# Joined bundles of small matmuls, and a table of steps for the scheduler's ranks, in a fused memory-attention and feed-forward kernel

## The chip, the cores and the metric

The kernel runs on one core of one Trainium2 chip. The metric is the device time of one execution in microseconds (us), the median of several runs. Five engines matter: TensorE (PE in the profile; PEld is its weight load), VectorE (DVE), ScalarE (ACT), GpSimd (POOL) and the queue that issues DMAs (SP).

## What is computed

```python
a = phi - max(phi, axis=seq); a = exp(a); a = a / sum(a, axis=seq)
k_m = einsum('bhsm,bhsd->bhmd', a, k)          # 32 memories per head
v_m = einsum('bhsm,bhsd->bhmd', a, v)
scores = softmax(q @ k_m.T / sqrt(64), axis=m)
x = scores @ v_m                               # then heads side by side: 4608 x 512
h = x @ w_in                                   # 512 -> 2048
g = h * erf(softplus(h))
out = g @ w_out                                # 2048 -> 512
```

There are 8 batches, 8 heads, 576 positions, 64 numbers per head, 32 memories; all is float32.

## The kernel before

**The work and its steps.** Since `scores @ v_m @ w_in` can be grouped the other way, the kernel never forms `x`: it multiplies `v_m` by `w_in` first. Per batch there are these kinds of work on PE. `sums` (in `one_memory`, L548) are 40 matmuls that make `k_m` and `v_m` of a batch (80, in two bundles, in batch 0); a transposition (`turn`, L582) follows. `heads` (L605) makes two things out of 64-row, 32-column pieces: `scores` of one half of a batch's positions (`attention`, two per batch, 8 matmuls of 288 columns) and `vw`, that is `v_m` times 512 columns of `w_in` (four per batch, 8 matmuls of 512 columns; eight of 256 columns in batch 0). These three are the *small* bundles; they are exact float32, and each of their matmuls stands twice in the profile. The wide work is `ffn1` (L710: one half of 288 positions of one 128-row slice of `h`, 6 matmuls) and `ffn2` (L794: one 128-row tile of the output, 3 matmuls for each of 16 slices of `g`). A *step* is one slice of `h`; there are 16 per batch, 128 in all. 64 positions of each batch do not fill a tile of 128; they go through DRAM (`rest_d`) and two batches' rests make one tile, `psr` (`ffn2_rest`).

**Numbers in two parts.** Most products are float32 in three passes, with each operand split into a high and a low part (`split`, L360: ACT writes the high part, DVE subtracts for the low part, `vw_lo`, `at_lo`, `wo`). The first steps use exact float32 matmuls instead: ffn1 in the first 4 steps (`psh<-at`), ffn2 in the first 8 (`pso<-w`).

**Around PE.** ffn1's result goes from PSUM to `h` by a copy of DVE (L725; ACT may take it in the first 16 steps, L726). ACT makes softplus and erf in groups of steps, each with a table load (L733, L738). DVE multiplies `e` and `h` and splits the product into `g` (`g_split`, L748, L764, L765). In the startup the weights are decoded (`decode`: a cast, L447; a scaling on ACT, L448, or DVE, L450; a merge, L442) from a packed form. PSUM has four tiles `ps`, which small bundles, transpositions, ffn1 and `psr` share (a `vw` or `scores` bundle takes two, `sums` one, an ffn1 half one), and four for the output.

**Who sets the order.** The program is first recorded as operations (`Plan.op`) with an engine, a planned cost, what they read and write, and a rank, 100 times a step plus an offset. `Plan.order` then plays them through: whenever an engine is free it takes, among the operations that are ready within 100 ns and whose tiles fit, the one of lowest rank. On PE, while a small bundle runs, another that is ready goes first:

```python
near = [x for x in can if x.ready <= t0 + self.NEAR]
if e == PE and small and any(x.kind == "small" and x.ready <= t0 for x in near):
    near = [x for x in near if x.kind == "small" and x.ready <= t0]
...
x = min(near, key=lambda x: x.rank)
```

The order found is issued as it is; each engine runs its instructions in that order and waits by semaphores. While PE would idle in the startup, `fill` (L369) issues matmuls of zeros.

Of the kernel before, what the change touches and what calls it, by code (L numbers as in the profile page):

```python
# [39 lines left out]


class Op:
    def __init__(self, ways, rank, kind, nbytes, edge):
# [25 lines left out]
class Plan:  # L69
# [7 lines left out]
    NEAR = 100.0  # L77
    AHEAD, WORTH = 0.0, 0.4

# [5 lines left out]
    def tile(self, pool, *key):  # L85
# [3 lines left out]
        return key  # L89

    def op(self, engine, cost, rank, reads, writes, emit, kind=None, nbytes=0, edge=None, after=(),
           holds=(), other=()):
        x = Op({engine: (cost, emit), **dict(other)}, rank, kind, nbytes, edge)
        x.before.update(after)
        for w, keys in ((False, reads), (True, writes)):
            for k in keys:
                k, part = (k[0], k[1]) if isinstance(k[0], tuple) else (k, None)
                x.tiles.add(k)
                for q, (wrote, read) in self.seen.setdefault(k, {}).items():
                    if q == part or q is None or part is None:  # L100
                        x.before.update(wrote)
                        if w:
                            x.before.update(read)
        for w, keys in ((False, reads), (True, writes)):
            for k in keys:
                k, part = (k[0], k[1]) if isinstance(k[0], tuple) else (k, None)
                s = self.seen[k]
                if w and part is None:
                    s.clear()
                wrote, read = s.setdefault(part, ([], []))  # L110
                if w:
                    wrote[:] = [x]
                    read.clear()
                else:
                    read.append(x)
        x.before.discard(x)
        for k in x.tiles:
            if k in self.users:
                self.users[k].append(x)
                x.placed.append(k)  # L120
        x.placed += [k for k in holds if k not in x.tiles]
        self.ops.append(x)
        return x

    def order(self):
        n_wait = {}
        for x in self.ops:
            n_wait[x] = len(x.before)
            for y in x.before:
                y.after.append(x)  # L130
# [3 lines left out]
        free = dict.fromkeys(ENGINES, 0.0)  # L134
# [3 lines left out]

        def fits(x):
            need = {}  # L140
            for k in x.placed:
                if k in held:
                    continue
                p = self.pool_of[k]
                if p not in self.any_order and self.turn[p][turn[p] + need.get(p, 0)] != k:
                    return False
                need[p] = need.get(p, 0) + 1
            return all(room[p] >= n for p, n in need.items())

# [3 lines left out]
        while len(out) < len(self.ops):  # L153
            best = None
            for e, xs in waiting.items():
                can = [x for x in xs if fits(x)]
                if e == ACT and not at_edge:
                    can = [x for x in can if x.kind != "exp"]
                can = [x for x in can if len(x.ways) == 1 or best_way(x) == e]
                if not can:  # L160
# [3 lines left out]
                if e == PE and small and any(x.kind == "small" and x.ready <= t0 for x in near):  # L164
                    near = [x for x in near if x.kind == "small" and x.ready <= t0]
                elif e in (ACT, DVE) and self.AHEAD:
                    near = [x for x in can if x.ready <= t0 + self.AHEAD]
                    near = [min(near, key=lambda x: x.rank + self.WORTH * max(0.0, x.ready - t0))]
                x = min(near, key=lambda x: x.rank)
# [67 lines left out]
def tile_memory_attention_then_erf_softplus_ffn(  # L237
# [36 lines left out]
    GROUPS = [4] * 4 + [6] * 18 + [2, 2]  # L274
    LAG = 8
    assert sum(GROUPS) == NS
    FR1, FR2 = 4, 8
# [262 lines left out]
    def one_memory(rank, b, part):  # L540
# [28 lines left out]
        cost = n_g * NC * (220 if b else 110)  # L569
        op(PE, cost, rank, [a] + kvs, [ps], sums, kind="small", holds=[t])  # L570
        for n, g in enumerate(gs):
# [16 lines left out]
        for par in range(2):  # L588
            rows = slice(par * D, (par + 1) * D)
            for i, x in enumerate(xs):  # L590
# [3 lines left out]
                def emit(rows=rows, par=par, i=i, dst=dst, x=x):  # L594
# [8 lines left out]
                   [((name, b % 2), (g, par)) for g in gs], emit)  # L603

    def heads(rank, reads, w, x, n, holds, *key):  # L605
        ps = [tile_("ps", "psa", *key, par, shape=[P, n], pool="ps") for par in range(2)]
# [12 lines left out]

        op(PE, 4 * n / 2.4, rank, reads, ps, emit, kind="small", holds=holds)  # L620
        return ps
# [225 lines left out]
    def at(step):  # L847
        return 100 * step

    second, split_at, ends = {}, {}, []  # L850
    for n in GROUPS:
        first = ends[-1] + 1 if ends else 0
        ends.append(first + n - 1)
        for k in range(first, first + n):
            near = n == 2 and k < NS // 2
            split_at[k] = max(ends[-1] + 1, k + (2 if near else n))
            second[k] = k + (3 if near else n + 2)

    TOGETHER = [tuple((g, x) for g in range(NG) for x in range(2))]
    EARLY = [tuple((g, x) for g in range(NG)) for x in range(2)]  # L860
# [15 lines left out]

    memories(at(-10), at(-9), 0, EARLY)
    decode(at(-3), "in", 0)
    for u in range(2):
        attention(at(-8), at(-7 + 2 * u), u)  # L880
    vw(at(-5), 0, 0, 1, FR1 > 0)

# [32 lines left out]
    for b in range(1, B, 2):  # L915
        for k in range(0, NK, 2):
            n = (b + 1) * NK + k // 2 if b < B - 1 else max(second[NS - NK + k + 1] + 1, NS)
            if b < B - 1:
# [11 lines left out]
    for i in range(NS + LAG + 4):  # L930
# [3 lines left out]
        for f, args in sorted(todo.get(i, ()), key=lambda t: t[0] in (ffn2, ffn2_rest)):  # L934
            f(*args)
        if i < NS:
# [63 lines left out]
```

## Time and profile before

| | |
|---|---|
| time, median of 3 runs | 714.97 us (714.64 to 716.32) |
| the profiled execution | 716.53 us, of which the span is 714.4 us |
| PE busy | 702.5 us, 98% of the span, 4883 matmuls |
| DVE busy | 509.8 us, 71%, 950 instructions |
| ACT busy | 393.9 us, 55%, 608 instructions |
| granted clock of TensorE | full (2.4 GHz) in all 40 slices of the span |

The profiled execution lies 1.56 us above the median of the runs; 2.1 us of it lie outside the span. Matmuls overlap in the records, so in the list in order of time the distance from one start to the next is what counts, not the length. Where a row holds several matmuls, its length is that of all of them. `psa` are the small bundles' PSUM tiles, `psh` those of ffn1, `pso` and `psr` those of ffn2.

### The profile page before, as it was taken

How to read it: one execution, taken by the hardware profiler on the slowest of the kernel's cores; microseconds unless marked ns; L12 is line 12 of the kernel's file. 1: busy time of each engine (PE TensorE's matmuls, PEld its weight loads, DVE VectorE, ACT ScalarE, POOL GpSimd, SP SyncE). 2: the span in 40 equal slices, each digit the busy share in tenths (PEclk: the TensorE clock that was granted, in tenths of full speed). 3: DMA queues.
4: the chain of work that ended last, by engine and by line, in shares of the span. 5: the costliest groups of instructions: out<-in, count | busy, mean ns of one | idle time of the engine just before them, and what ended most of it. 6: DMA issues, size and time to landing. Idle time of an engine off the chain costs nothing.

```text
span 714.4 us, 12285 instructions
## 1 busy us (share of the span) xinstructions
PE 702.5 (98%) x4883; PEld 557.3 (78%) x4883; DVE 509.8 (71%) x950; ACT 393.9 (55%) x608; POOL 29.6 (4%) x70
## 2 busy tenths in 40 slices
PE   7999999999999999999999999999999999999997
PEld 3565668788878888887887888888887888888885
DVE  3899999898546967869647786967756486874730
ACT  4799986767514473654716482653825264463701
POOL 0011110000000000000000000000000000011320
PEclk9999999999999999999999999999999999999999
DMA  8999975545532646262354635253433233310002
GB/s 321 416 408 404 408 245 196 187 150 169 182 118 86 192 125 230 74 213 90 130 190 135 210 110 180 95 177 122 138 100 114 90 96 89 93 49 31 0 1 73
DMA packets 66664, 114.95 MB, mean 161 GB/s; under 512 B 37552, under 2 KB 45744, under 8 KB 62512
## 3 DMA queue, kind: packets, MB, share of 16 engines
q1 hardware_dynamic: 66608, 114.18, 46.2%
q8 instruction: 38, 0.62, 0.3%
q14 instruction: 18, 0.15, 0.1%
HBM read 93.19 MB, written 20.97 MB: 160 GB/s over the span
## 4 chain that ended last, share of the span: by engine, by line
PE 91%; DMA 3%; DVE 3%; ACT 2%; SPq 1%; issue 0%; ACTq 0%; DVEq 0%
PE pso L794 49%; PE psh L710 28%; PE psr L794 6%; PE psa L612 6%; PE psa L560 2%; DMA q<-qT 2%; DMA rest_d<-g 1%; ACT w L448 1%; DVE vw_lo L364 0%; SPq L401 0%; PE psa L582 0%; DVE w L447 0%; DVE h L725 0%; DVE at_lo L364 0%; PE psa L489 0%
## 5 line engine op out<-in xcount | busy, mean ns | idle before, releaser
L794 PE MATMUL pso<-wo,g 128*128 128x512 f32 x1440 | 356.4, 394 | 0.0
L794 PEld LDWEIGHTS pso<-wo,g 128*128 128x128 f32 x1440 | 262.1, 188 | 59.5 <-issue 7.4
L733 ACT ACTIVATE e<-h 128x576 f32<-128x576 f32 x128 | 86.3, 683 | 185.0 <-DVE h L725 184.5
L725 DVE COPY h<-psh 128x288 f32<-128x288 f32 x238 | 105.6, 450 | 27.6 <-PE psh L710 26.0
L764 DVE CAST g<-e 128x576 fp32r<-128x576 f32 x120 | 54.3, 453 | 86.6 <-PE pso L794 76.5
L710 PE MATMUL psh<-at_hi,vw_hi 128*128 128x288 f32 x496 | 110.8, 305 | 0.2 <-DVE vw_lo L364 0.2
L710 PE MATMUL psh<-at_hi,vw_lo 128*128 128x288 f32 x496 | 106.2, 295 | 0.4 <-DVE vw_lo L364 0.4
L710 PE MATMUL psh<-at_lo,vw_hi 128*128 128x288 f32 x496 | 106.1, 295 | 0.0
L710 PEld LDWEIGHTS psh<-at_hi,vw_hi 128*128 128x128 f32 x496 | 84.6, 188 | 27.5 <-issue 5.6
L748 DVE TENSOR_TENSOR e<-e,h 128x576 f32<-128x576 f32 x120 | 87.7, 750 | 15.2 <-ACT e L738 15.2
L765 DVE TENSOR_TENSOR g<-e,g 128x576 fp32r<-128x576 f32 x120 | 90.2, 752 | 1.7
L738 ACT ACTIVATE e<-e 128x576 f32<-128x576 f32 x128 | 80.4, 675 | 0.3
L710 PEld LDWEIGHTS psh<-at_hi,vw_lo 128*128 128x128 f32 x496 | 79.8, 188 | 0.6 <-DVE vw_lo L364 0.6
L710 PEld LDWEIGHTS psh<-at_lo,vw_hi 128*128 128x128 f32 x496 | 79.1, 188 | 0.0
L362 ACT ACTIVATE vw_hi<-psa 128x512 fp32r<-128x512 f32 (+1 forms) x68 | 35.2, 554 | 42.9 <-PE psa L612 42.6
L364 DVE TENSOR_TENSOR vw_lo<-psa,vw_hi 128x512 fp32r<-128x512 f32 (+1 forms) x68 | 42.3, 635 | 11.8 <-ACT vw_hi L362 11.7
L794 PE MATMUL psr<-wo,rr 128*128 128x512 f32 x192 | 49.1, 392 | 0.0
L794 PEld LDWEIGHTS psr<-wo,rr 128*128 128x128 f32 x192 | 36.1, 188 | 7.9
L774 POOL CAST rr<-g 128x64 fp32r<-128x64 f32 x32 | 17.4, 553 | 585.5 <-DVE g L764 580.3
L841 ACT ACTIVATE ot<-pso 128x512 f32<-128x512 f32 x32 | 18.6, 591 | 40.7 <-PE pso L794 33.8
L612 PE MATMUL psa<-wi,vm 64*32 64x512 f32 (+1 forms) x576 | 37.1, 553 | 0.2 <-DVE ssm L669 0.2
L794 PE MATMUL pso<-w,g 128*128 128x512 f32 x64 | 29.8, 600 | 1.8 <-DVE g L748 1.8
(72 smaller groups left out, 507.9 us busy)
## 6 DMA issues: line engine op xcount, KB each, us to landing
wi<-w_in_d SPq DMA_DIRECT2D x28, 1024.0 KB, 5.3
kv<-kv SPq DMA_DIRECT2D x32, 640.0 KB, 8.4
q<-qT SPq DMA_DIRECT2D x16, 576.0 KB, 6.6
out<-ot SPq DMA_DIRECT2D x32, 256.0 KB, 2.1
w<-w_in SPq DMA_DIRECT2D x8, 1023.8 KB, 14.4
w<-w_out SPq DMA_DIRECT2D x8, 1023.8 KB, 15.6
rr<-rest_d SPq DMA_DIRECT2D x28, 256.0 KB, 2.9
rest_d<-g SPq DMA_DIRECT2D x104, 64.0 KB, 2.2
```

The lines of the kernel that those rows point to most:

```text
L362: lambda: nc.scalar.activation(get_hi(), get_src(), AF.Identity))
L364: lambda: nc.vector.tensor_tensor(out=get_lo(), in0=get_src(), in1=get_hi().bitcast(F32), op=ALU.subtract))
L612: nc.tensor.matmul(out=get(ps[par])[p * M : (p + 1) * M, :], lhsT=w()[rows, p, :], rhs=x()[rows, p, :], start=True, stop=True,)
L710: nc.tensor.matmul(out=get(ps), lhsT=x[:, g, k % 4 * P : (k % 4 + 1) * P], rhs=y[:, g, :], start=(n + g == 0), stop=(n == len(parts) - 1 a ...
L725: lambda: nc.vector.tensor_copy(out=keep(), in_=get(ps)),
L733: last[:] = [op(ACT, on_act(S), rank, [("h", i)], [e], lambda: nc.scalar.activation(get(e), get(("h", i)), AF.Softplus), kind="softplus", ...
L738: last[:] = [op(ACT, on_act(S), rank, [e], [e], lambda: nc.scalar.activation(get(e), get(e), AF.Erf), kind="erf", edge=edge, after=last)]
L748: op(DVE, on_dve(S), rank, [e, h], [to if i >= FR2 else (t, 0)], lambda: nc.vector.tensor_tensor(out=get(t)[:, 0].bitcast(F32) if i < FR2 ...
L764: op(DVE, on_dve(S, 1), rank, [e], [(t, 0)], lambda: nc.vector.tensor_copy(out=get(t)[:, 0], in_=get(e)))
L765: op(DVE, on_dve(S), rank, [e, (t, 0)], [(t, 1)], lambda: nc.vector.tensor_tensor(out=get(t)[:, 1], in0=get(e), in1=get(t)[:, 0].bitcast(F ...
L794: nc.tensor.matmul(out=o, lhsT=y, rhs=z, start=(start and n == 0), stop=(stop and n == len(parts) - 1))
L841: lambda: nc.scalar.activation(get(t)[:, :DM], get(o), AF.Identity))
```

## The change

Four things change in how the order is found; what is computed, and with which instructions, stays.

1. **Joins.** An operation may be appended to an earlier one (`join`): it gets no place of its own, the first operation takes its reads, writes and cost, the higher of the two ranks, and issues both, one right behind the other. From batch 2 on the first `vw` of a batch is joined to the `sums` of the next batch (5 times), and each of the two `scores` of batch b to the third or fourth `vw` of batch b - 1 (10 times, from batch 3).
2. **Held-up bundles.** While a small bundle is ready and only lacks tiles of the pool `ps`, PE takes no other operation of higher rank that needs a new tile of that pool.
3. **A table** `SHIFT` of 64 entries adds a number of steps, -14 to 14, to the rank of all that one call records (`call`): single calls in the first batches, and one entry for all later batches where its key begins with "s".
4. The rest tile of batches 0/1, 2/3 and 4/5 is multiplied from ten steps later on, in four steps instead of eight. A setting (`AHEAD`) that was 0 is dropped.

```diff
+SHIFT = {
...
+    "decode": {
+        ("in", 1): -9, ("in", 2): -8.5, ("in", 3): -1.5, ("out", 0): -13.5, ("out", 1): -2.5, ("out", 3): -4.5,
...
     def op(self, engine, cost, rank, reads, writes, emit, kind=None, nbytes=0, edge=None, after=(),
-           holds=(), other=()):
-        x = Op({engine: (cost, emit), **dict(other)}, rank, kind, nbytes, edge)
+           holds=(), other=(), join=None):
+        x = join or Op({engine: (cost, emit), **dict(other)}, rank, kind, nbytes, edge)
+        if join:
+            (was, first), x.rank = x.ways[engine], max(x.rank, rank)
+            x.ways[engine] = (was + cost, lambda: (first(), emit()))
+        else:
+            x.shift = self.shift
...
         for x in self.ops:
+            x.rank += 100 * x.shift
...
+                if e == PE:
+                    t0 = max(free[e], now)
+                    held_up = [x.rank for x in xs if x.kind == "small" and x.ready <= t0
+                               and not fits(x) and fits(x, self.any_order)]
+                    if held_up:
+                        first = min(held_up)
+                        can = [x for x in can if x.kind == "small" or x.rank < first or not any(
+                            k not in held and self.pool_of[k] in self.any_order for k in x.placed)]
...
+    JOIN = 2
...
-        op(PE, cost, rank, [a] + kvs, [ps], sums, kind="small", holds=[t])
+        small["sums", b] = op(PE, cost, rank, [a] + kvs, [ps], sums, kind="small", holds=[t])
...
+    small = {}
+
+    def partner(what, b, c=0):
+        if what == "vw":
+            return small["sums", b + 1] if c == 0 and JOIN <= b < B - 1 else None
+        u = b
+        return small["vw", u // 2 - 1, 4 + 2 * (u % 2)] if u // 2 > JOIN else None
...
-        op(PE, 4 * n / 2.4, rank, reads, ps, emit, kind="small", holds=holds)
+        small[key] = op(PE, 4 * n / 2.4, rank, reads, ps, emit, kind="small", holds=holds, join=partner(*key))
...
+    def call(f, *args):
+        name, key = f.__name__, args[2 if f in (memories, attention) else 1 :]
+        key = tuple(x for x in key if isinstance(x, (int, str)))
...
+        plan.shift = SHIFT.get(name, {}).get(key, 0)
+        f(*args)
+        plan.shift = 0
...
-            n = (b + 1) * NK + k // 2 if b < B - 1 else max(second[NS - NK + k + 1] + 1, NS)
+            n = (b + 1) * NK + 10 + k // 4 if b < B - 1 else max(second[NS - NK + k + 1] + 1, NS)
...
-            f(*args)
+            call(f, *args)
```

**In the order, first place: PE, the last `vw` and `scores` before batch 7.** Here `psa<-wi,vm` is a `vw` bundle and `psa<-q,km` a `scores` bundle. Before, the fourth `vw` of batch 6:

```order
L794 MATMUL pso<-wo,g 128x512 x12
L794 MATMUL psr<-wo,rr 128x512 x6
L612 MATMUL psa<-wi,vm_103 32x512 x8
L710 MATMUL psh<-at_hi,vw_hi 128x288 x2
L710 MATMUL psh<-at_lo,vw_hi 128x288 x2
L710 MATMUL psh<-at_hi,vw_lo 128x288 x2
```

and, further on, the second `scores` of batch 7:

```order
L710 MATMUL psh<-at_hi,vw_hi 128x288 x2
L710 MATMUL psh<-at_lo,vw_hi 128x288 x2
L710 MATMUL psh<-at_hi,vw_lo 128x288 x2
L612 MATMUL psa<-q,km_102 32x288 x8
L794 MATMUL pso<-wo,g 128x512 x12
```

After the change both in one place:

```order
L769 MATMUL psh<-at_lo,vw_hi 128x288 x2
L769 MATMUL psh<-at_hi,vw_lo 128x288 x2
L853 MATMUL pso<-wo,g 128x512 x6
L671 MATMUL psa<-wi,vm_103 32x512 x8
L671 MATMUL psa<-q,km_102 32x288 x8
L853 MATMUL pso<-wo,g 128x512 x6
L769 MATMUL psh<-at_hi,vw_hi 128x288 x2
```

The `scores` bundle moved up to the `vw` bundle, and both moved in between output matmuls: two ways into small matmuls and out of them became one.

**Second place: PE, the `sums` of batch 7 (`psa<-kv,phi`) and the first `vw` of batch 6.** Before, the `sums` stand between output matmuls and ffn1, and that `vw` fifteen rows earlier:

```order
L710 MATMUL psh<-at_hi,vw_lo 128x288 x2
L794 MATMUL pso<-wo,g 128x512 x12
L560 MATMUL psa<-kv,phi 32x128 x40
L710 MATMUL psh<-at_hi,vw_hi 128x288 x2
L710 MATMUL psh<-at_lo,vw_hi 128x288 x2
L710 MATMUL psh<-at_hi,vw_lo 128x288 x2
```

After the change:

```order
L769 MATMUL psh<-at_hi,vw_lo 128x288 x2
L611 MATMUL psa<-kv,phi 32x128 x40
L671 MATMUL psa<-wi,vm_103 32x512 x8
L853 MATMUL pso<-wo,g 128x512 x9
L671 MATMUL psa<-wi,vm_103 32x512 x8
L853 MATMUL pso<-wo,g 128x512 x3
L769 MATMUL psh<-at_hi,vw_hi 128x288 x2
```

The first `vw` follows the `sums` with nothing between. Both come right behind ffn1 now, and nine output matmuls, the second `vw` and three more output matmuls stand between them and the next ffn1.

**Third place: DVE and PE in the startup.** DVE, from the reciprocal of the second `scores` to the low parts of the first split `vw` (`w_133` and `w_139` are the third and fourth part of the packed `w_in`, `w_130` the first of `w_out`). Before:

```order
L671 RECIPROCAL srs_442<-ssm_413 128x18
L447 CAST w_133<-w_133 128x1024
L672 TENSOR_TENSOR sc_367<-sc_367,srs_442 128x576
L442 SCALAR_TENSOR_TENSOR wi_449<-w_133 128x4x256
L679 STREAM_TRANSPOSE at_462<-sc_367 128x576
L364 TENSOR_TENSOR at_lo_484<-at_396,at_hi_464 128x576
L447 CAST w_130<-w_130 128x1024
L364 TENSOR_TENSOR at_lo_497<-at_462,at_hi_486 128x576
L364 TENSOR_TENSOR vw_lo_503<-psa_469,vw_hi_489 128x256
L364 TENSOR_TENSOR vw_lo_503<-psa_471,vw_hi_489 128x256
```

After:

```order
L730 RECIPROCAL srs_427<-ssm_413 128x18
L493 SCALAR_TENSOR_TENSOR w_130<-w_130 128x1024
L731 TENSOR_TENSOR sc_367<-sc_367,srs_427 128x576
L498 CAST w_133<-w_133 128x1024
L738 STREAM_TRANSPOSE at_468<-sc_367 128x576
L493 SCALAR_TENSOR_TENSOR wi_474<-w_133 128x4x256
L415 TENSOR_TENSOR at_lo_486<-at_396,at_hi_470 128x576
L498 CAST w_139<-w_139 128x1024
L784 COPY h_423<-psh_483 128x288
L501 TENSOR_SCALAR w_139<-w_139 128x1024
L415 TENSOR_TENSOR vw_lo_516<-psa_495,vw_hi_510 128x256
L415 TENSOR_TENSOR vw_lo_516<-psa_497,vw_hi_510 128x256
```

The merge of `w_130` and the cast and scaling of `w_139` moved ahead of `vw_lo`, the second `at_lo` moved behind it, and the cast of `w_130` moved up to stand ahead of these rows. PE, the last 256-wide `vw` of that stretch and the first output matmuls (`pso<-w`). Before:

```order
L710 MATMUL psh<-at_lo,vw_hi 128x288 x2
L710 MATMUL psh<-at_hi,vw_lo 128x288 x2
L612 MATMUL psa<-wi,vm_103 32x256 x8
L794 MATMUL pso<-w,g 128x512
L710 MATMUL psh<-at_hi,vw_hi 128x288 x2
```

After, where that `vw` comes first and ffn1 of steps 4 to 7 fills the rows between it and these:

```order
L769 MATMUL psh<-at_hi,vw_hi 128x288 x2
L769 MATMUL psh<-at_lo,vw_hi 128x288 x2
L769 MATMUL psh<-at_hi,vw_lo 128x288 x2
L853 MATMUL pso<-w,g 128x512 x16
L671 MATMUL psa<-wi,vm_103 32x256 x8
```

The first output matmuls moved behind four more halves of ffn1, those of steps 6 and 7, and sixteen of them now stand in a row.

## Rows read from the trace of the kernel before

**Rows 1.** The page: the span, and busy us, share and instructions of each engine.
```profile
span 714.4 us, 12285 instructions
...
PE 702.5 (98%) x4883; PEld 557.3 (78%) x4883; DVE 509.8 (71%) x950; ACT 393.9 (55%) x608; POOL 29.6 (4%) x70
```

**Rows 2.** Busy us (count) by stretch: PE, PEld, DVE, ACT, POOL; clock, DMA share.
```profile
37.00:100.00 63.00, 60.86 (x451) 38.48 (x457) 60.76 (x93) 58.07 (x91) 9.68 (x20) 1.00 0.97 378
...
190.00:690.00 500.00, 499.81 (x3307) 412.11 (x3306) 344.43 (x662) 251.13 (x383) 14.28 (x26) 1.00 0.36 118
```

**Rows 3.** Waits of PE's matmuls, 36 to 710 us: us in total, times, longest.
```profile
PE pso L794 <- DVE g L748: 1.8, 1, 1.8
PE psh L710 <- DVE vw_lo L364: 0.6, 2, 0.4
```

**Rows 4.** PE in time: start, length, instructions; a lone `vw` bundle.
```profile
477.92 2.23 PE L794 MATMUL pso<-wo,g 128*128 128x512 f32 x9
480.07 1.09 PE L612 MATMUL psa<-wi,vm 64*32 64x512 f32 x16
481.09 0.96 PE L794 MATMUL pso<-wo,g 128*128 128x512 f32 x3
481.90 0.43 PE L710 MATMUL psh<-at_hi,vw_hi 128*128 128x288 f32 x2
```

**Rows 5.** PE in time: a lone `vw` bundle that waited.
```profile
327.84 2.68 PE L794 MATMUL pso<-wo,g 128*128 128x512 f32 x11
330.45 2.10 PE L612 MATMUL psa<-wi,vm 64*32 64x512 f32 x16
332.49 0.53 PE L710 MATMUL psh<-at_hi,vw_hi 128*128 128x288 f32 x2
```

**Rows 6.** PE in time: a lone `scores` bundle.
```profile
212.33 0.71 PE L612 MATMUL psa<-q,km 64*32 64x288 f32 x16
212.97 1.65 PE L794 MATMUL pso<-wo,g 128*128 128x512 f32 x6
```

**Rows 7.** PE in time: `vw`, then `scores`.
```profile
401.93 1.09 PE L612 MATMUL psa<-wi,vm 64*32 64x512 f32 x16
402.81 0.69 PE L612 MATMUL psa<-q,km 64*32 64x288 f32 x16
403.43 0.98 PE L794 MATMUL pso<-wo,g 128*128 128x512 f32 x3
```

**Rows 8.** PE in time: a lone `sums` bundle.
```profile
170.22 2.40 PE L560 MATMUL psa<-kv,phi 116*32 116x128 f32 x80
172.54 0.97 PE L794 MATMUL pso<-wo,g 128*128 128x512 f32 x3
```

**Rows 9.** PE in time: `sums`, then `vw`.
```profile
348.68 2.40 PE L560 MATMUL psa<-kv,phi 116*32 116x128 f32 x80
351.00 1.09 PE L612 MATMUL psa<-wi,vm 64*32 64x512 f32 x16
352.02 0.97 PE L794 MATMUL pso<-wo,g 128*128 128x512 f32 x3
```

**Rows 10.** Groups by line and shape: count, busy us, mean ns of one.
```profile
L733 ACT ACT_TABLE_LOAD x24 | 30.8, 1283 | 0.4
...
L447 DVE CAST w<-w 128x1024 f16<-128x1024 bf16 x16 | 21.1, 1332 | 0.0
...
L442 DVE SCALAR_TENSOR_TENSOR w<-w 128x1024 uint32<-128x1024 uint32 x8 | 9.8, 1225 | 0.6 <-ACT w L448 0.6
...
L364 DVE TENSOR_TENSOR at_lo<-at,at_hi 128x576 fp32r<-128x576 f32 x2 | 1.6, 786 | 0.0
L450 DVE TENSOR_SCALAR w<-w 128x1024 int32<-128x1024 uint32 x2 | 1.4, 716 | 0.0
```

**Rows 11.** DVE and PE in time, startup: the first split `vw`, and its reader.
```profile
33.54 0.77 DVE L364 TENSOR_TENSOR vw_lo<-psa,vw_hi 128x256 fp32r<-128x256 f32 x2
...
36.83 0.64 PE L710 MATMUL psh<-at_hi,vw_hi 128*128 128x288 f32 x2
```

More of the change, by code (lines that the diff above doesn't have):

```diff
@@ L37 @@
 }
+SHIFT = {
+    "at_split": {
+        (0,): -6,
+    },
+    "attention": {
+        ("s", 0): -12, (0,): -13, (1,): -13, (4,): 10, (5,): 2.5,
+    },
+    "decode": {
+        ("in", 1): -9, ("in", 2): -8.5, ("in", 3): -1.5, ("out", 0): -13.5, ("out", 1): -2.5, ("out", 3): -4.5,
+        ("out", 5): -8, ("out", 6): 8.5,
+    },
+    "ffn2_rest": {
+        (7, 10, 2): -5,
+    },
+    "g_split": {
[3 rows of a table added]
+    },
+    "load_kv": {
+        (2, 0, 1): 11.5,
+    },
+    "memories": {
+        ("s",): 1, (1,): 2, (2,): 1,
+    },
+    "split_wo": {
+        (1,): -14, (3,): -7, (4,): 3, (7,): 10.5,
+    },
[5 rows of a table added]
+    },
+}
 class Op:
@@ L77 @@
     NEAR = 100.0
-    AHEAD, WORTH = 0.0, 0.4
     def __init__(self, room, any_order):
@@ L89, in tile @@
         return key
+    shift = 0
     def op(self, engine, cost, rank, reads, writes, emit, kind=None, nbytes=0, edge=None, after=(),
-           holds=(), other=()):
-        x = Op({engine: (cost, emit), **dict(other)}, rank, kind, nbytes, edge)
+           holds=(), other=(), join=None):
[5 more added lines that the diff above has]
+            x.shift = self.shift
         x.before.update(after)
@@ L117, in op @@
         for k in x.tiles:
-            if k in self.users:
+            if k in self.users and x not in self.users[k]:
                 self.users[k].append(x)
@@ L121, in op @@
         x.placed += [k for k in holds if k not in x.tiles]
-        self.ops.append(x)
+        if not join:
+            self.ops.append(x)
         return x
@@ L137, in order, with fits @@
         releases, out, now, held = [], [], 0.0, set()
-        def fits(x):
+        def fits(x, but=()):
             need = {}
@@ L147, in fits @@
                 need[p] = need.get(p, 0) + 1
-            return all(room[p] >= n for p, n in need.items())
+            return all(room[p] >= n for p, n in need.items() if p not in but)
         def best_way(x):
@@ L165, in order @@
                     near = [x for x in near if x.kind == "small" and x.ready <= t0]
-                elif e in (ACT, DVE) and self.AHEAD:
-                    near = [x for x in can if x.ready <= t0 + self.AHEAD]
-                    near = [min(near, key=lambda x: x.rank + self.WORTH * max(0.0, x.ready - t0))]
                 x = min(near, key=lambda x: x.rank)
@@ L857, in tile_memory_attention_then_erf_softplus_ffn @@
             second[k] = k + (3 if near else n + 2)
+    STEADY = ("load_wi", "load_phiT", "load_phi", "load_kv", "memories")
     TOGETHER = [tuple((g, x) for g in range(NG) for x in range(2))]
@@ L875, in tile_memory_attention_then_erf_softplus_ffn @@
     load_weight(at(2 * NPR - 11), "out", NPR - 1)
-    memories(at(-10), at(-9), 0, EARLY)
-    decode(at(-3), "in", 0)
+    def call(f, *args):
+        name, key = f.__name__, args[2 if f in (memories, attention) else 1 :]
+        key = tuple(x for x in key if isinstance(x, (int, str)))
+        if name in ("g_split", "quad") and key[0] >= 48:
+            key = ("s", key[0] % NK)
+        elif name in ("attention", "load_q") and key[0] >= 6:
+            key = ("s", key[0] % 2)
+        elif name in STEADY and key[0] >= 3:
+            key = ("s", *key[1:])
+        elif name in ("ffn2_rest", "load_rest") and key[0] < B - 1:
+            key = ("s", *key[1:])
+        plan.shift = SHIFT.get(name, {}).get(key, 0)
+        f(*args)
+        plan.shift = 0
+    call(memories, at(-10), at(-9), 0, EARLY)
+    call(decode, at(-3), "in", 0)
     for u in range(2):
-        attention(at(-8), at(-7 + 2 * u), u)
-    vw(at(-5), 0, 0, 1, FR1 > 0)
+        call(attention, at(-8), at(-7 + 2 * u), u)
+    call(vw, at(-5), 0, 0, 1, FR1 > 0)
     todo = {}
```

8 rows, old and new, of the table SHIFT are left out of this document.

## The prediction

> **What bounds the kernel now.** I read four views, in this order. First the page's sums: TensorE (PE) is busy for 702.5 of the span's 714.4 us [rows 1]. Busy time alone proves little, because matmul records overlap; so, second, busy time by stretch [rows 2]: from 190 to 690 us PE is busy for 499.81 of 500 us while VectorE (DVE) is busy for 344, so DVE has room there; from 37 to 100 us PE shows 60.86 of 63 us, DVE 60.76 and ScalarE (ACT) 58.07, so there two more engines are nearly full. Third, PE's waits after the startup: one of 1.8 us for a `g` of DVE, and 0.6 us for `vw_lo` [rows 3]. Fourth, PE in order of time, where distances from start to start are what PE really spends. Nine 512-wide matmuls of the output product and the way into a bundle take 480.07 - 477.92 = 2.15 us [rows 4], eleven of them 330.45 - 327.84 = 2.61 [rows 5]: two more cost 0.46, so 0.23 each. Only what comes on top of such a stream can be saved, and the bundles of small matmuls come on top.
>
> **What a bundle costs, alone and joined.** A lone `vw` bundle runs from 480.07 to 481.09, 1.02 us; the nine matmuls ahead of it take 2.15 us where nine times 0.23 is 2.07 (0.08 to enter), the three behind it 0.81 where 0.69 is due (0.12 to get going again) [rows 4]. So entering and leaving cost 0.20, and alone it costs 1.22 us. A lone `scores` bundle is 0.64 us from its start to the next matmul [rows 6], 0.84 with the same 0.20. Joined, `vw` and `scores` last 0.88 + 0.62 = 1.50 us [rows 7], 1.70 with one entry and exit. The join saves 1.22 + 0.84 - 1.70 = 0.36; I take 0.35. A lone `sums` bundle lasts 2.32 us [rows 8], and `sums` followed by `vw` 2.32 + 1.02 = 3.34 [rows 9]: nothing is saved at the seam, only one entry and exit, 0.20.
>
> The two kinds of join differ in the shape that the rows print, 64\*32 for `vw` and `scores`, 116\*32 for `sums`. The Trainium skill, TensorEngine Tiling (Array Packing), section Key Properties, says that changing the tiling mode, and not just the tile, drains TensorE. By that rule a join of `sums` with `vw` keeps its seam; the trace agrees as far as the seam goes (2.32 + 1.02, no less than apart), but entry and exit are still saved once. If the rule were taken to leave such joins worthless, the sum below would be 0.8 us smaller; the measured 0.20 decides.
>
> **The change, term by term.**
> 1. *Joins.* In the order of before I count 51 groups of small matmuls between wide ones, in that of the change 39. Neighbours of `vw` and `scores` go from 6 to 12: 6 x 0.35 = 2.1 us. `sums` next to a 512-wide `vw` goes from 2 to 6: 4 x 0.20 = 0.8 us. Two pairs of `vw` of the last batch now stand next to each other, which the trace does not show. Below, such a pair saves nothing; above, what `vw` with `scores` saves, 0.35. The shapes are equal (64\*32), so I take the upper end: 0.7 us. The twelve groups fewer give **3.6 us** (2.9 with the low end). All of it lies on PE, and PE is the path wherever it runs without a gap [rows 2].
> 2. *The wait of 1.8 us for the first `g`.* Before, PE finishes the last 256-wide `vw` and then waits for the first `g` [rows 3]. Now ffn1 of steps 6 and 7 (four halves, 24 matmuls) stands ahead of that `g`, so PE has something to run. Against this, DVE's queue ahead of the first non-exact `vw_lo` gains one merge (1.23), one cast (1.33) and one scaling (0.72) and loses one `at_lo` (0.79) [rows 10]: 2.5 us more. That `vw_lo` ended at 33.54 + 0.77 = 34.3 us, and PE used it only at 36.8, since it still had exact ffn1 to do [rows 11]; this swallows the 2.5 us almost exactly. Eight non-exact halves in a row also need eight evacuations from four PSUM tiles, while ACT loads a function table in between (1.28) [rows 10]. So the gain lies between 1.8 (nothing takes its place) and a loss of 0.7 (the 2.5 us of DVE on the path less 1.8). I take 1.8 less one table load, **0.5 us**.
> 3. *The longer wait for `vw_lo`, 0.4 us* [rows 3]. PE meets it at step 16, the first of batch 1, whose `vw` stood three output matmuls and one ffn1 half ahead. Now 33 output matmuls stand between them, so **0.4 us** goes. The bounds are 0 and 0.4.
> 4. *Other waits in the steady part.* One `vw` bundle took 2.04 us where 1.02 is due [rows 4, 5]: it waited 1.0 us for a PSUM tile whose copy stood behind other work in DVE's queue. Such accidents depend on the order of DVE, which changes everywhere. I expect as many as before: **0**. Bounds: all gone, 1.0 + 0.2 gained; or one in each of the 20 joined bundles at the 0.2 us that one of six joined bundles showed [rows 3] (its shorter wait), 4 us lost.
> 5. *The rest.* `ffn2_rest` of batches 1, 3 and 5 starts ten steps later and is done in four steps instead of eight. The matmuls are the same, and their PSUM tile is held for a shorter time. Their loads on the sync queue move with them; DMA has a share of 0.36 from 190 to 690 us [rows 2], so 0, unless a load lands behind its reader, and then PE has output matmuls of other tiles to run. Two fillers more (61 for 59) lie in the startup, where PE waits anyway: 0. The shifted decoding in the startup moves weight stores and loads past each other on the sync queue, and POOL's memsets keep their order: 0, covered by the 63 us in which output matmuls on exact weights keep PE busy; if that cover fails, the second rival below is the price. The tail keeps its order (output product, a last `psr`, ACT's copy, two stores), with 6 instead of 12 `psr` matmuls at the end and as many in all: 0.
>
> Sum: 3.6 + 0.5 + 0.4 = 4.5 us. The profiled execution took 716.53 us, so 712.0 for an execution like it. It lies 1.56 above the median of the runs, 714.97; 4.5 below that median is **710.5 us**, my forecast. About 0.3% (2.1 us) is what a measurement of this kernel can tell from no change.
>
> **The rivals.**
> - *Every wait goes too.* PE would then run from 37 us without a gap: 3.6 + 1.8 + 0.4 + 1.2 = 7.0, **708.0 us**. For it: PE's recorded waits in that part are few, and short. Against it: DVE and ACT are 92% to 96% busy up to 100 us [rows 2], and an order written for planned durations meets real ones. Chance 0.13.
> - *DVE becomes the bound early.* The 2.5 us that move ahead of `vw_lo` do not fit into the slack, and everything up to 100 us is late by them, since DVE has 2.2 us free of 63 [rows 2]: 3.6 + 0.4 - 0.7 = 3.3 if nothing else comes, and up to 2.5 us more lost at each further place where the order of DVE is too tight. With one such place 0.8 is left: **714.2 us**, inside 0.3%. Against it: `g` 8 to 11 now stand earlier in DVE's queue against what PE has ahead of them. Chance 0.16, with all else that ends within 0.3%.
> - *Evacuation eats the joins: slower.* A joined `vw` with `scores`, or `vw` with `vw`, writes all four tiles of the pool `ps`. Nothing of ffn1 can start until ACT and DVE have emptied one, and before the bundle PE may run nothing new that takes a tile (the new rule for held-up bundles). The place is the first ffn1 behind, or the second half inside, each of 20 joined bundles. Price 0.2 us as seen once, 1.0 as at the bundle of [rows 5]. It decides from 4.5 / 20 = 0.23 us a bundle; at 0.4 the loss is 8 - 4.5 = 3.5 and the time **718.5 us**. Against it: five of the six joined bundles of before, some with ffn1 right behind, show no wait [rows 3], and behind 15 of the 20 stand six or more output matmuls (1.4 us) before the next ffn1. Chance 0.09. The Trainium skill, TensorEngine Tiling (Array Packing), section PSUM Bottleneck, warns of just this: tiling speeds up TensorE but not PSUM evacuation, so the copies may become the bottleneck. By that rule the time would be this rival's; the joined bundles of before are too few to exclude it.
> - *The change does not do what it says.* The order shows the joins, so only their worth can fail; with nothing from the two `vw` pairs it would be 711.2. It lies within the forecast's range.
>
> **How the numbers follow.** The forecast, between 2.1 and 6 us gained, has 0.62; all waits gone 0.13; little left 0.16; slower 0.09. Faster by over 0.3% is 0.62 + 0.13 = 0.75, the same 0.16, slower 0.09. The range reaches from the first rival, 708.0, less 0.9 us for waits that hide in PE's weight loads, 707.1, up to 714.2, the second rival. Outside it lie the slower case and about a tenth of the others.
>
> **What would show it.** After the change the timeline of PE should show `vw` and `scores` as neighbours twelve times, at 1.5 us from the first start to the next wide matmul; `sums` and `vw` at 3.3; the first `g` used without a wait, near 45 us; PE's waits past 37 us at about 1 to 2 us in total; and the last matmul some 4 us earlier with the tail behind it unchanged. I am wrong if the joined bundles or the first ffn1 behind them are longer by more than 0.2 us on average, if DVE's `g` or `vw_lo` ends PE's waits between 37 and 100 us for more than 3 us, or if the joins are all there and cheap and the time has still not moved.

## The result, and the profile after

The changed kernel takes **708.22 us** (median of 6 runs, 707.81 to 709.55); the kernel before, run beside it, 715.60 (714.64 to 717.24). The ratio is 0.9896, with a 95% interval of 0.9882 to 0.9910: 7.4 us less. The forecast was 710.5, 4.5 us less than before, in a range from 707.1 to 714.2; what came is nearly the rival "Every wait goes too" (708.0). The profiled execution took 707.81 us and shows 8.4 us less span than that of before, which lay 1.56 above its median.

The page after, the lines that answer to [rows 1]:

```profile
span 706.0 us, 12251 instructions
...
PE 698.4 (99%) x4885; PEld 559.8 (79%) x4885; DVE 508.5 (72%) x944; ACT 395.9 (56%) x616; POOL 30.9 (4%) x70
```

Busy us by stretch, after, in the columns of [rows 2]:

```profile
37.00:100.00 63.00, 63.00 (x438) 40.92 (x438) 60.03 (x91) 57.56 (x96) 12.09 (x20) 1.00 0.99 375
190.00:690.00 500.00, 500.00 (x3317) 417.27 (x3316) 343.26 (x659) 246.93 (x375) 17.31 (x32) 1.00 0.36 118
```

PE has no gap left in either stretch (60.86 and 499.81 before). The view of PE's waits, which had two rows before the change [rows 3], now lists none at all between 36 and 702 us. DVE and ACT did not get less full: 60.03 and 57.56 of 63 us.

PE in order of time, with the one DVE row of the first split `vw` (start, length, instructions), after:

```profile
35.51 0.76 DVE L415 TENSOR_TENSOR vw_lo<-psa,vw_hi 128x256 fp32r<-128x256 f32 x2 [0.24 <-ACT vw_hi L413]
36.08 0.64 PE L769 MATMUL psh<-at_hi,vw_hi 128*128 128x288 f32 x2
...
36.83 0.43 PE L769 MATMUL psh<-at_hi,vw_lo 128*128 128x288 f32 x2
...
43.25 0.42 PE L769 MATMUL psh<-at_hi,vw_lo 128*128 128x288 f32 x2
43.51 2.74 PE L853 MATMUL pso<-w,g 128*128 128x512 f32 x6
...
382.68 1.09 PE L671 MATMUL psa<-wi,vm 64*32 64x512 f32 x16
383.56 0.69 PE L671 MATMUL psa<-q,km 64*32 64x288 f32 x16
384.18 1.21 PE L853 MATMUL pso<-wo,g 128*128 128x512 f32 x4
...
425.36 2.40 PE L611 MATMUL psa<-kv,phi 116*32 116x128 f32 x80
427.69 1.09 PE L671 MATMUL psa<-wi,vm 64*32 64x512 f32 x16
428.71 1.65 PE L853 MATMUL pso<-wo,g 128*128 128x512 f32 x6
...
605.86 1.95 PE L671 MATMUL psa<-wi,vm 64*32 64x512 f32 x32
607.73 0.97 PE L853 MATMUL pso<-wo,g 128*128 128x512 f32 x3
```

Three things are to be seen. The joined bundles cost what [rows 7, 9] said: 384.18 - 382.68 = 1.50 us for `vw` with `scores`, 428.71 - 425.36 = 3.35 for `sums` with `vw`. The pair of `vw` that no row of before showed runs 607.73 - 605.86 = 1.87; entry and exit included (measured, for every group, as the distance from the wide matmul before it to one behind it, less what the stream of wide ones takes) it costs 2.10, and two lone ones 2 x 1.22: **0.34 saved**. And the first `g` is used at 43.51 without a wait.

Where 8.4 us of the profiled executions went, by distances from start to start:

| from | us |
|---|---|
| 12 groups fewer: 6 x 0.34 + 4 x 0.20 + 2 x 0.34 | 3.5 |
| the wait for the first `g` | 1.8 |
| two waits for `vw_lo`, at 99 and 277 us (0.55, 0.36) | 0.9 |
| `vw` at 330 us that waited [rows 5], and 0.1 at another | 1.1 |
| first split ffn1 earlier, 36.83 to 36.08; 0.35 of it because loads landed earlier, 0.40 by the order | 0.75 |
| sum (the last matmul starts at 701.15 for 709.54, 8.39 earlier) | 8.05 |

The last term has two causes. The first exact ffn1 starts 0.35 us earlier (23.79 for 24.14); this is when its loads landed, and not the change: that start lies between 22.8 and 25.5 us in the traces with the startup of before, and between 22.7 and 24.5 in those with the table's. The distance from there to the first split ffn1 is 12.67 to 12.69 us in all six traces with the startup of before, and 12.28 to 12.33 in the eight with the table's. In the first kind PE stands 0.65 to 0.68 us at about 34 us, for the first of the two `vw_lo`; a trace with the table's startup has no such wait. Here is the one of before, just ahead of the stretch that [rows 3] lists:

```profile
34.03 3.18 PE L710 MATMUL psh<-at,vw_hi 128*128 128x288 f32 x12 [0.65 <-DVE vw_lo L364]
```

### The profile page after: what moved, and what is told of

Its sections match the earlier page's. It is cut to its first block, busy times and chain, and to the rows that moved or that the text cites. A ratio compares the mean times of both kernels' runs of the same rounds, so it can differ in the third digit from the quotient of the medians.

```text
span 706.0 us, 12251 instructions
## 1 busy us (share of the span) xinstructions
PE 698.4 (99%) x4885; PEld 559.8 (79%) x4885; DVE 508.5 (72%) x944; ACT 395.9 (56%) x616; POOL 30.9 (4%) x70
## 4 chain that ended last, share of the span: by engine, by line
PE 96%; DMA 2%; SPq 1%; DVE 0%; ACT 0%; issue 0%
PE pso L853 51%; PE psh L769 29%; PE psr L853 6%; PE psa L671 6%; PE psa L611 2%; DMA q<-qT 2%; PE psa L633 0%; PE idle L424 0%; SPq L452 0%; PE psa L540 0%; DVE sc L717 0%; SPq L443 0%; ACT sc L725 0%; DVE sc L722 0%; DVE sc L731 0%
## 5 line engine op out<-in xcount | busy, mean ns | idle before, releaser
L784 DVE COPY h<-psh 128x288 f32<-128x288 f32 x230 | 102.0, 452 | 36.6 <-PE psh L769 35.5
L769 PE MATMUL psh<-at_hi,vw_hi 128*128 128x288 f32 x496 | 108.0, 299 | 0.0
L797 ACT ACTIVATE e<-e 128x576 f32<-128x576 f32 x128 | 78.7, 676 | 0.3
L415 DVE TENSOR_TENSOR vw_lo<-psa,vw_hi 128x512 fp32r<-128x512 f32 (+1 forms) x68 | 41.1, 631 | 10.8 <-ACT vw_hi L413 10.6
L671 PE MATMUL psa<-wi,vm 64*32 64x512 f32 (+1 forms) x576 | 35.6, 553 | 0.0
```

What stands on the lines that cost most here:

```text
L415: lambda: nc.vector.tensor_tensor(out=get_lo(), in0=get_src(), in1=get_hi().bitcast(F32), op=ALU.subtract))
L671: nc.tensor.matmul(out=get(ps[par])[p * M : (p + 1) * M, :], lhsT=w()[rows, p, :], rhs=x()[rows, p, :], start=True, stop=True,)
L769: nc.tensor.matmul(out=get(ps), lhsT=x[:, g, k % 4 * P : (k % 4 + 1) * P], rhs=y[:, g, :], start=(n + g == 0), stop=(n == len(parts) - 1 a ...
L784: lambda: nc.vector.tensor_copy(out=keep(), in_=get(ps)),
L797: last[:] = [op(ACT, on_act(S), rank, [e], [e], lambda: nc.scalar.activation(get(e), get(e), AF.Erf), kind="erf", edge=edge, after=last)]
```

## The experiments

All were timed in five rounds beside the kernel before (715.66, 716.52, 716.02 and 715.84 us in the four sessions); ratios are to it. Group costs are taken as above.

### Taking the joins apart, one kind at a time

The second half of a joined pair is issued behind the next output tile instead of right behind the first half, for the ten joined `scores` (first kernel) or four of the joined `sums` (second, the condition shown; `parts` are the two halves):

```diff
-        x.emit()
+        if hasattr(x, "parts") and any(k[:3] == ("psa", "kmvm", b) for k in x.tiles for b in (4, 5, 6, 7)):
+            x.parts[0]()
+            held = x.parts[1]
+        else:
+            x.emit()
+            if held and x.engine == PE:
+                held()
+                held = None
```

> The changed kernel, with each of its ten joined pairs of vw and scores taken apart at the very end: the scores bundle is issued one output tile (three matmuls) after its vw, everything else in the same order. Groups of small matmuls go from 39 to 49. Theory A (a group costs one entry and one exit, whatever is in it; a pair apart costs 0.34 us more): 10 x 0.34 = 3.4 us slower than the changed kernel, 711.6 us, and no wait of PE comes or goes. Rival B (the gain lies in the order of DVE and ACT that the table found, the seam is hidden anyway): no change, 708.2. Rival C (four PSUM tiles taken at once delay ffn1): apart is faster than joined, below 708.2.

> The changed kernel, with the four joined pairs of sums and vw that are followed by an output tile taken apart in the same way: vw is issued one output tile after sums. Groups go from 39 to 43. Theory A: the seam between the two shapes costs the same as leaving and entering in part, so 4 x 0.20 = 0.8 us slower, 709.0. Rival: joining saves the same as for scores, 4 x 0.34 = 1.4, 709.6; or nothing, 708.2. In the trace the gap is read directly: sums to vw 2.32, then vw alone 1.02 with its own entry and exit.

Measured: 713.55 us for the `scores`, ratio 0.9968 (0.9954 to 0.9982), 5.3 more than the changed kernel; 709.45 for the `sums`, 0.9910 (0.9894 to 0.9926), 1.2 more. In the first the costs of all groups from 36 us on rise by 5.0 us, from 61.6 to 66.6: ten seams, and two places where ffn1 stood right behind a late `scores` and waited (these two groups cost 1.55 us each where 0.85 is usual), by PE's waits from 36 us on:

```profile
PE psh L770 <- DVE sc L718: 1.3, 2, 0.6
```

So 3.6 us for ten seams, and 1.4 that theory A did not have: the latter is the wait of the "evacuation" rival, which a joined bundle with output matmuls behind it does not meet. In the second, `sums` 2.53 and `vw` 1.23 apart against 3.56 together: 0.20 each, as in [rows 8, 9]. By distances from start to start, three places behind the moved bundles lose 0.17, 0.17 and 0.39 us more, which makes up the rest; the list of waits shows only one of them (0.2). **The prices of the joins hold.**

### The table, the joins and the rest tile, each left out

No table, all else kept:

```diff
-SHIFT = {
...
+SHIFT = {}
```

> The changed kernel with an empty table: joins, the rule for held-up bundles and the later rest tile stay. Counted in its order: 43 groups, 11 neighbours of vw and scores (12 with the table), 5 of sums and a 512-wide vw (6), no pair of vw (2). Theory A (the table's own part is that PE's waits go: about 4 of the 7.4 us): 0.34 + 0.20 + 2 x 0.33 = 1.2 us for the groups and 3 to 4.5 us for waits that are back, 712.5 to 714. Rival (the joins and the rule free PE, the table adds little): 1.2 us alone, 709.4.

712.62 us, 0.9951 (0.9933 to 0.9970): as expected. PE's waits, 36 to 710 us:

```profile
PE pso L819 <- DVE g L773: 1.8, 1, 1.8
PE psh L735 <- DVE vw_lo L381: 0.4, 1, 0.4
```

The waits at the start are back, those of the steady part are not: the table is worth 4.4 us. Of it 3.1 lie ahead of 100 us: these two waits, and 0.9 by which split ffn1 starts later (36.96 us for 36.08). About half of the 0.9 is when the loads landed, so some 2.6 us are the order's there.

No joins, all else kept:

```diff
-    JOIN = 2
+    JOIN = 99
```

> The changed kernel with no operation appended to another: table, rule for held-up bundles and later rest tile stay. Counted in its order: 45 groups, 7 neighbours of vw and scores (12 with joins), 5 of sums and a 512-wide vw (6), two pairs of vw (2). Theory A: 5 x 0.34 + 0.20 = 1.9 us for the groups; the table was written for the order with joins, so waits of up to 2 us may come: 710.1 to 712. Rival (the table holds without the joins, and joined bundles only take tiles away from ffn1): 708.2 or less.

716.24 us, 1.0002 (0.9990 to 1.0015): no gain at all, where 710.1 to 712 was expected. The groups cost 1.9 us more, as priced. PE's list of waits adds 5.0, which the table brings when the bundles don't stand where it was written for; about 1 us of the 8.0 was not placed. The longest two:

```profile
PE psa L671 <- DMA q<-qT: 2.9, 2, 1.6
PE pso L853 <- ACT ot L900: 1.7, 2, 0.9
```

This was the first run that the theory "each part pays its own seams and waits" missed, so the next ones put in one part alone.

Joins alone (the kernel before with `join` and `partner`, nothing else):

> Kernel before plus the joins alone (no table, no rule for held-up bundles, rest tile as before). Order: 42 groups of small matmuls for 51; vw with scores 12 for 6, sums with a 512-wide vw 5 for 2. Prices measured so far: 0.34 us for a vw with scores, 0.20 for a sums with vw. Theory A (the joins pay only their seam, and the waits for the first g and vw_lo belong to the startup's order, which the joins don't touch): groups 6 x 0.34 + 3 x 0.20 = 2.6 us, wait for g of 1.8 us still there. The waits of 1.0 and 0.36 us in the steady part were gone in the kernel without the table; if the joins took them away, 1.4 more: 715.6 - 4.0 = 711.6 us; if the later rest tile did, 713.0. Rival B (joins need the table's order to pay, as the table needs the joins): no faster than 715.0.

715.77 us, 0.9987 (0.9973 to 1.0002), where 711.6 to 713.0 was expected: rival B. The later rest tile alone:

```diff
-            n = (b + 1) * NK + k // 2 if b < B - 1 else max(second[NS - NK + k + 1] + 1, NS)
+            n = (b + 1) * NK + 10 + k // 4 if b < B - 1 else max(second[NS - NK + k + 1] + 1, NS)
```

> Kernel before plus only the rest tile ten steps later and in four steps. The order of before is then already one in which 11 scores bundles stand right behind a vw (6 before), with 46 groups for 51, since the psr tile is held for a shorter time. Theory A (what counts is that the bundles are neighbours, not that they are joined): 5 x 0.34 = 1.7 us, 713.9 us, and 712.5 if the two waits of the steady part go as well. Rival B (the rest tile is worth nothing by itself): 715.6 us.

716.88 us, 1.0018 (0.9992 to 1.0043): no faster either. Both have the bundles and their prices (`vw` with `scores` 1.72 in every case), and a wait that eats them. PE's waits, joins alone:

```profile
PE psa L498 <- ACT bias L492: 1.9, 1, 1.9
PE pso L811 <- DVE g L765: 1.8, 1, 1.8
PE psa L629 <- DVE sc L675: 0.6, 1, 0.6
PE psh L727 <- DVE vw_lo L373: 0.4, 1, 0.4
```

and the rest tile alone, the first row:

```profile
PE psr L794 <- DMA rr<-rest_d: 3.4, 1, 3.4
```

The chain behind the 1.9 us, joins alone, in order of time (SP, then DVE, ACT, PE):

```profile
397.37 0.35 SPq L401 DMA_DIRECT2D phiT<-phiT  x1
397.76 0.47 SPq L860 DMA_DIRECT2D out<-ot  x1
398.33 0.53 SPq L786 DMA_DIRECT2D rest_d<-g  x1
399.20 0.33 SPq L410 DMA_DIRECT2D kv<-kv  x1
399.59 0.41 SPq L470 DMA_DIRECT2D wi<-w_in_d  x1
401.02 0.33 SPq L401 DMA_DIRECT2D phiT<-phiT  x1
...
408.89 0.75 DVE L485 TENSOR_REDUCE pmx<-phiT 128x1 f32<-128x576 f32 x1 [3.09 <-DMA phiT<-phiT]
409.74 0.69 ACT L492 ACTIVATE bias<-ident,pmx 128x128 f32<-128x128 f32 x2 [3.22 <-DVE pmx L487]
...
410.19 0.62 PE L498 MATMUL psa<-ident,bias 128*128 128x128 f32 x2 [1.92 <-ACT bias L492]
```

The second half of the next batch's `phiT` is issued behind two stores, a load of `kv` and one of `wi`; it lands 8 us later, and DVE, ACT and PE stand in turn, each in its fixed order.

Joins and the later rest tile together, no table, no rule:

> Kernel before plus the joins and the later rest tile, without the table and without the rule for held-up bundles. Order: 43 groups, 11 vw with scores, 5 sums with a 512-wide vw. The kernel with the rule as well ran in 712.62, that with the joins alone in 715.77 us, each with the wait of 1.8 us for the first g. Theory A (the rule is what keeps the joins free of waits when there is no table): 714 to 717 us. Rival B (the later rest tile does): 712.6 us.

712.81 us, 0.9942 (0.9922 to 0.9962): rival B. Only the 1.8 and 0.4 at the start are left, as without the table. So it is the later rest tile that frees the joins of new waits. The rule for held-up bundles changes no time there (712.62 with it), though some operations stand elsewhere. In the changed kernel it moves nothing at all: without it the program has the same order on every engine.

Table and joins, but the rest tile where it was (that line taken back):

> Kernel after with the rest tile of batches 0/1, 2/3 and 4/5 multiplied as before (ten steps earlier, in eight steps). Order: the same 39 groups and neighbours as after. Theory A (the groups pay, and the rest tile by itself is worth nothing): 708.2 us. Rival B (the table was fitted to the rest tile's place too, and without it waits come, as with the joins taken out): 710 to 714 us.

**730.42 us**, 1.0192 (1.0170 to 1.0215), 22 more than the changed kernel, though the 39 groups are the same. PE's longest waits, then SP and DVE in time:

```profile
PE psh L769 <- DVE pmx L529: 5.2, 1, 5.2
PE pso L853 <- DVE g L823: 3.0, 1, 3.0
PE psa L540 <- ACT bias L534: 3.0, 1, 3.0
```

```profile
392.37 0.52 SPq L443 DMA_DIRECT2D phiT<-phiT  x1
392.94 0.47 SPq L902 DMA_DIRECT2D out<-ot  x1
393.51 0.52 SPq L452 DMA_DIRECT2D kv<-kv  x1
394.09 0.44 SPq L512 DMA_DIRECT2D wi<-w_in_d  x1
395.82 0.33 SPq L443 DMA_DIRECT2D phiT<-phiT  x1
...
403.31 0.75 DVE L527 TENSOR_REDUCE pmx<-phiT 128x1 f32<-128x576 f32 x1 [5.55 <-DMA phiT<-phiT]
403.98 0.45 DVE L784 COPY h<-psh 128x288 f32<-128x288 f32 x1
```

The same chain: here DVE stands for 5.55 us with copies of `h` queued behind it, and ffn1 finds no PSUM tile. PE's waits sum to 14.8 us in all. After the long ones the granted clock was 0.50 for some 17 us, by stretch (busy us of PE, PEld, DVE, ACT, POOL, then clock and DMA share) the longer part:

```profile
402.40:412.40 10.00, 4.94 (x19) 4.51 (x20) 7.85 (x17) 7.88 (x12) 0.00 (x0) 0.50 0.01 2
```

PE was busy for 10.6 us of that time in both parts; at the full level of the clock half of it would do, by my estimate 5 us lost. With the waits that is about 20 of the 22 us.

The copy `ot` of the rest tile's output (`store`, L898) uses one of the two tiles `phiT` that the next batch's load wants; with the rest tile late it comes when those loads are done. To test that, the rest tile's copy got a tile of its own (which also moves operations on PE, DVE, ACT and SP, since the order is found anew):

```diff
-        t = tile_("h" if final else "phiT", "ot", *o)
+        t = tile_("h" if final else "rot" if o[0] == "psr" else "phiT", "ot", *o)
```

> The kernel with the rest tile where it was (730.42 us), but with a tile of its own for the copy of the rest tile's output; there it shares the two tiles phiT with the next batch's phi, whose load stood between the two stores of that copy and behind them. PE's order is the same but for some output matmuls and one bias transposition. Theory A (the 22 us come from that shared tile: the load of phiT is issued late, DVE waits 5.5 us for it with copies of h behind it, and PE 5.4 and 3.3 us for these): the waits near 231 and 399 to 409 us go, with them the stretches at the lower clock behind them; 709 to 716 us. Rival B (the rest tile's own place takes PSUM tiles or output matmuls from where the table needs them, whatever the loads do): 726 us or more.

723.89 us, 1.0101 (1.0074 to 1.0127): between both. The tile, with the order that it brings, is worth 6.5 of the 22 us. The loads still stand behind `kv` and `wi` (issued at 393.86 us); DVE waits 4.1 us for them, to 402.99, and the `g` that PE then waits for stands behind that in DVE's queue, at 406.87:

```profile
PE pso L854 <- DVE g L824: 8.0, 2, 6.6
PE psh L770 <- DVE sc L718: 2.7, 2, 2.1
```

Waits, and the low clock behind them, make up the other 15 us by size. What they hang on, the loads' order or the output matmuls that the early rest tile uses up, was not separated and **stays open**.

### The table in two halves

Only the 29 entries of the startup, and only the 35 others:

> Kernel after with only the 29 entries of the table that act in the startup (decoding, batch 0's attention and vw, the first g); joins, rule and rest tile kept. Order: 42 groups for 39, no vw next to a vw. Theory A (the startup entries take the waits for the first g and vw_lo away, and the other entries pay only the two vw pairs and a sums join): 708.2 + 0.66 + 0.2 = 709.1 us, no wait for g. Rival B (the 64 entries hold only together: the half of them moves bundles to places with new waits): 711 us or more.

> Kernel after with only the 35 other entries of the table. Order: 40 groups for 39, two vw pairs as in the kernel after. Theory A: the wait for the first g (1.8 us), that for vw_lo (0.6) and the later start of the first split ffn1 (0.9) are back, and one vw with scores is missing (0.34): 708.2 + 3.6 = 711.8 us. Rival B (the waits at the start go by the entries that hold for all later batches): under 710 us.

709.56 us, 0.9898 (0.9877 to 0.9918), for the first: theory A, with no wait for the first `g` (0.8 and 0.2 us of other waits). 715.94, 0.9990 (0.9976 to 1.0003), for the second, 4.1 over theory A. The wait of the startup for the first `g` (1.8, the second row) is back, and there are new ones from 100 to 145 us, the longest in the first row:

```profile
PE pso L824 <- DVE g L795: 1.9, 2, 1.6
PE pso L824 <- DVE g L778: 1.8, 1, 1.8
```

So the startup entries carry the table. The others gain 1.3 us on top of them, the two `vw` pairs above all, and do harm alone (715.94 for 712.62 without any table).

### A version that was to beat the change

The second `vw` of a batch joins the first, instead of the first joining the `sums`:

```diff
-            return small["sums", b + 1] if c == 0 and JOIN <= b < B - 1 else None
+            return small["vw", b, 0] if c == 2 and JOIN <= b < B - 1 else None
```

> A version meant to beat the kernel after: the first vw of batches 2 to 6 is joined by the second vw of its own batch instead of joining the sums of the next batch. Order: 39 groups as after, 7 pairs of vw (2 after), 2 sums with vw (7 after, one of them 256 wide), 12 vw with scores as after. Theory A (a join pays by its seam: 0.33 us for a vw pair, 0.20 for a sums with vw): 708.2 - 5 x 0.33 + 5 x 0.20 = 707.6 us. Rival B (the table fits one order only, and the first vw and second vw now need four PSUM tiles at once: waits of 1 to 4 us as in the kernels that had only a part of the change): 709.2 to 712 us.

724.85 us, 1.0110 (1.0089 to 1.0130). All seven pairs of `vw` cost 2.08 to 2.10 us but one, which met ffn1 right behind it. That one and two others of PE's waits:

```profile
PE psr L853 <- DMA rr<-rest_d: 5.2, 4, 1.7
PE pso L853 <- DVE g L823: 3.0, 1, 3.0
PE psh L769 <- ACT vw_hi L413: 1.7, 1, 1.7
```

The price was right again and worth nothing: 17 us more than the changed kernel, against 0.65 of seams. PE's waits are 10.8 of it; behind them the granted clock was 0.50 for 9.6 us of busy time between 385 and 413 us, by my estimate 5 us more. Here too DVE stood for `phiT`, 14.4 us.

## Why the prediction was right, and where its terms were not

The time lies in the range because the range was wide: the sum said 4.5 us, 7.4 came, and the range reached so far down only for a rival with a chance of 0.13. The joins came as priced. On top of the sum, in the profiled executions, came waits that it left standing (1.3 us for `g`, 1.5 of others) and 0.4 us of the startup's order that no term had; 0.35 more came by earlier loads, which is not the change. So the mechanism of the joins was right, and that the time lies in the range is luck for the rest.

**Joins (term 1): right.** 3.6 forecast, 3.5 measured. Taking the upper end for the `vw` pairs was right: 0.34 for 0.35. The Trainium skill, TensorEngine Tiling (Array Packing), section Key Properties, has a change of the tiling mode drain TensorE; this agrees with what the runs show of the three kinds of seam: 0.34 saved between equal shapes (64\*32), 0.20 between 116\*32 and 64\*32.

**First `g` (term 2): mis-sized.** The step that failed is "1.8 less one table load". All 1.8 us came. That `vw_lo` would not be waited for held: the second ended at 36.27 for 34.31, and its first reader, the third matmul pair at 36.83, did not wait. But the reason was misread. The row at 36.83 in [rows 11] reads `vw_hi`, and PE had no slack ahead of it: it stood 0.65 us for the first `vw_lo`, at 34.03. In the traces with the table's startup neither wait shows, and the stretch of exact ffn1, in another order, is 0.40 us shorter; no term had that. Eight evacuations and a table load were priced as a wait, but from 36.08 to 43.51 no row shows one.

**Longer `vw_lo` wait (term 3): right.** 0.4 taken, 0.55 gone.

**Other steady waits (term 4): wrong.** I expected as many as before, 0; all went, 1.1 + 0.36 = 1.5 us. The step took waits for accidents at a steady rate. They are a property of the whole order: none past 100 us in the changed kernel or with joins and the later rest tile, but by the list of waits 3 to 15 us (without that for the first `g`) with joins alone, the rest tile alone, no joins, or the rest tile as before.

**The rest (term 5): the right number for a reason that fell.** I put the moved rest tile at 0 because DMA's share is 0.36 and PE would have other matmuls to run behind a late load. The runs show the contrary: behind a late load PE stood for 1.9 to 5.2 us, because its order is fixed. And this part is no 0: without it the other parts are worth -0.1% (joins) or cost 2% (joins and table). In the full change it cost nothing, and kept the rest free of waits.

**The rivals.** "Every wait goes too" had 0.13 and came; what I held against it, that DVE and ACT are nearly full and an order for planned durations meets real ones, did not bite, though both are as full as before. "DVE becomes the bound early": no, PE has no gap from 37 to 100 us. "Evacuation eats the joins" is a true mechanism in the wrong place: 0.6 us where ffn1 follows a late `scores`, 1.7 behind a `vw` pair, nothing in the changed kernel, where output matmuls stand behind all eleven `vw` bundles followed by `scores` and behind both `vw` pairs. That also bounds the rule of the Trainium skill, TensorEngine Tiling (Array Packing), section PSUM Bottleneck: it holds here only where no other work lies between the bundle and the next taker of a tile.

## What to carry to other kernels

Price a seam in the rows, from the wide matmul before a bundle to one behind it: such prices held to 0.03 us in every kernel here, where no wait fell in. Waits don't add up by parts in a kernel with a fixed order on every engine: joins, rest tile and table gave -0.1% (joins), +0.2% (rest tile), -0.6% (both), 0.0% (table and rest tile), +1.9% (table and joins) and -1.0% (all), so judge an order by its whole list of waits, and write a table last, for the final order. Look for the load that a tile shared with a store holds back on the SP queue; here a tile of its own for that store, with the order that it brought, gave back 6.5 of 22 us.

## What the runs showed of the hardware that was not expected

A wait of PE can cost more than itself. Joins alone, by stretch (busy us of PE, PEld, DVE, ACT, POOL, then clock and DMA share):

```profile
408.00:411.50 3.50, 1.58 (x9) 1.06 (x8) 2.58 (x7) 0.69 (x2) 0.00 (x0) 1.00 0.01 4
411.50:415.00 3.50, 3.50 (x10) 2.68 (x9) 2.15 (x3) 3.20 (x4) 0.00 (x0) 0.51 0.12 26
415.00:420.00 5.00, 5.00 (x48) 3.12 (x46) 2.35 (x9) 4.95 (x9) 0.00 (x0) 1.00 0.00 0
```

After the wait the granted clock is 0.51, the level of 1.2 GHz, for 3.5 us, with PE fully busy; eight 512-wide matmuls then come 0.20 us further apart each, 1.6 us on top of the 1.9. The same followed the wait of 3.4 us with the rest tile alone (0.50 for 2.5 us) and the long ones with the rest tile as before, whose mean clock is 0.987. The length of the wait does not settle it. With the 35 entries the clock fell behind the wait of 1.8 us for the first `g`, which ended at 41.4 us:

```profile
41.80:45.20 3.40, 3.40 (x12) 2.61 (x11) 3.40 (x5) 3.37 (x4) 0.97 (x2) 0.50 1.04 424
```

The same wait left it at 1.00 in five other traces, that of before among them, and the wait of 1.6 us with the 35 entries did too. What decides was not found. No term of the prediction had a price for that.
